# Building the rounding tails of the fp32r weights: sums on TensorE in PSUM in place of three GpSimd steps

## The chip, the cores and the metric

One NeuronCore of a Trainium2 chip runs the kernel; the other cores are not used. The metric is the device time of one execution in microseconds, the median over several runs. A profile is one further execution of the same program, recorded by the hardware profiler, and has a time of its own.

## The reference

Attention over a pooled key/value image, then two feed-forward layers with different activations. The arrays come in as float64 or float32 as the host has them; the weights of the feed-forward layers reach the kernel as 64-bit numbers.

```
kv_flat = mean over 4x4 blocks of kv, @ w_sr        # 768 keys, k = v
a   = softmax(q @ k.T / sqrt(128));  x = a @ v      # 12288 queries of 128
h   = x @ moe_w_in    (128 x 2048);  g = elu(h);           x2 = g @ moe_w_out
h   = x2 @ moe2_w_in  (128 x 2048);  g = max(0.01 h, h);   y  = g @ moe2_w_out
```

## The kernel before, in words

Every product is made from three fp32r matmuls: an operand is held as a head (the value rounded to fp32r) and a tail (the rest, rounded to fp32r), and `mm3` (lines 86 to 89) adds head x head, head x tail and tail x head in PSUM. The 12288 queries are worked on in 24 chunks of 512. For a chunk there are four score tiles of 128 queries, softmax, a turn of the result, the product with the values (`values`, line 433, 18 matmuls), and then for each of the two layers eight units: `up` (six matmuls, 256 hidden features), the activation, the split into head and tail, `down` (six matmuls). In the traces these matmuls stand under lines 87, 88 and 89: `ps` is what `up` and the scores write, `py` what `down` writes.

The weights of the layers are turned from 64-bit words into head and tail on the chip, once, in 32 jobs of 128 x 256 values (`w_parts`, lines 181 to 241). Before, a job is ten steps on a staged tile `ws` of pairs of words (low word, high word): ScalarE takes the absolute value of the high word (`w_abs`, line 193); GpSimd clamps it (`w_bound`, 197); VectorE shifts it (`w_shift`, 203), puts the sign in (`w_sign`, 210) and takes out the power of two (`w_power`, 217); ScalarE converts and scales the low word (`w_low`, 223) and rounds the upper part to the head `wh` (`w_head`, 227); GpSimd multiplies the scaled low word by the power (`w_b`, 231), subtracts the head from the upper part (`w_rest`, 235) and adds the two into the tail `wl` (`w_tail`, 239). The three scratch tiles `v`, `m`, `a` of a job come from the pool `wt` with three buffers, the staged words from `ws` with four.

The order of all instructions from the attention on is written out by a planner at the end of the function (lines 531 to 802). A `step` has an engine, a planned length, the steps that it follows and a key; `take` and `give` name buffers. The planner begins, again and again, the step that can begin first by its own model of the five engines (ties go to the smaller key), and emits it. Each engine then works through its own instructions in that order. Weight jobs have keys six units ahead of the unit that needs them. Three PSUM places of two banks each (`ps`) are shared by score tiles, the turns of the first two chunks (`turn_early`, 413), `values` and `up`; the planner hands them out. The remaining two banks hold the outputs of `down` (`py`). The activation steps that matter here are `relu` (468), `elu_exp` (471), `elu` (475, VectorE), `elu_head` (481, GpSimd), `leaky_head` and `leaky` (487, 491, ScalarE) and `tail` (495, VectorE, writes `gl`); of the attention, `largest` (347), `expo` (354), `norm` (373, GpSimd) and `tail_e` (422, VectorE).

The planned lengths of the steps of a weight job stand in lines 565 to 574 (0.36 us for a ScalarE step, 0.66 us for each of the three GpSimd steps at the end).

Of the kernel before, what the change touches and what calls it, by code (L numbers as in the profile page):

```python
# [18 lines left out]
P = 128  # L19
CH = 512  # L20
S = 32
WP = 256
# [17 lines left out]
def pooled_attention_elu_leaky_kernel(  # L40
# [50 lines left out]
    def pool(name, bufs, **kw):  # L91
        return ctx.enter_context(tc.tile_pool(name=name, bufs=bufs, **kw))

    const = pool("const", 1)
    ident = const.tile([P, P], F32, name="ident")
    w_src = {"i1": w_in1, "o1": w_out1, "i2": w_in2, "o2": w_out2}
    w_hi = {}
    w_lo = {}
# [17 lines left out]
    d_p = pool("scratch", 4, space=bass.MemoryType.DRAM)  # L116
    xs_p = pool("xs", 2)
    ws_p = pool("ws", WS)
    wt_p = pool("wt", 3)
    ps_p = [pool(f"ps_{i}", 1, space=PSUM) for i in range(3)]  # L120
    ps_y = pool("ps_y", 2, space=PSUM)

# [37 lines left out]


    wjobs = [(k, p) for ks in (("i1", "o1"), ("i2", "o2")) for p in range(DFF // WP) for k in ks]
    wst, wt = {}, {}

    def load_w(i):
        k, p = wjobs[i]
# [14 lines left out]
    def w_parts(i):  # L181

        k, p = wjobs[i]
        pp, o = divmod(p * WP, CH)
        hi, lo = w_hi[k, pp][:, o:o + WP], w_lo[k, pp][:, o:o + WP]
        u = lambda x: x.bitcast(U32)

        def w_abs():
            v, m, a = wt[i] = [wt_p.tile([P, WP], F32, tag=x, name=x) for x in "vma"]
            nc.scalar.activation(out=v, in_=f(wst[i][:, :, 1]), func=AF.Abs)

        def w_bound():
            v, m, a = wt[i]
            nc.gpsimd.tensor_scalar(  # L197
                out=v, in0=v, scalar1=TOP, scalar2=LEAST, op0=ALU.min, op1=ALU.max
            )

        def w_shift():
            v, m, a = wt[i]
            nc.vector.tensor_scalar(  # L203
                out=u(a), in0=u(v), scalar1=3, scalar2=0x3FFFFFF8,
                op0=ALU.logical_shift_left, op1=ALU.bitwise_and,
            )

        def w_sign():
            v, m, a = wt[i]
            nc.vector.scalar_tensor_tensor(  # L210
                out=u(a), in0=wst[i][:, :, 1], scalar=0xC0000000, in1=u(a),
                op0=ALU.bitwise_and, op1=ALU.bitwise_or,
            )

        def w_power():
            v, m, a = wt[i]
            nc.vector.tensor_scalar(
                out=u(m), in0=u(a), scalar1=0xFF800000, scalar2=None, op0=ALU.bitwise_and
            )

        def w_low():
            v, m, a = wt[i]
            nc.scalar.activation(out=v, in_=wst[i][:, :, 0], func=AF.Copy, scale=2.0 ** -52)

        def w_head():
            v, m, a = wt[i]
            nc.scalar.activation(out=hi, in_=a, func=AF.Copy)

        def w_b():
            v, m, a = wt[i]  # L230
            nc.gpsimd.tensor_tensor(out=v, in0=v, in1=m, op=ALU.mult)  # L231

        def w_rest():
            v, m, a = wt[i]
            nc.gpsimd.tensor_tensor(out=a, in0=a, in1=f(hi), op=ALU.subtract)  # L235

        def w_tail():
            v, m, a = wt[i]
            nc.gpsimd.tensor_tensor(out=lo, in0=a, in1=v, op=ALU.add)  # L239

        return w_abs, w_bound, w_shift, w_sign, w_power, w_low, w_head, w_b, w_rest, w_tail

    with tc.tile_pool(name="kvp", bufs=1) as kvp, tc.tile_pool(name="sums", bufs=2) as sum_p:
        wsr = kvp.tile([P, C], F32, name="wsr")
        nc.scalar.dma_start(out=wsr, in_=w_sr)
        NL = kv_v.shape[1] // 2
        kvt = [kvp.tile([P, 2, CH], F32, name=f"kv_{i}") for i in range(NL)]
        load_q(0)  # L250
        for i in range(NL):
            nc.sync.dma_start(out=kvt[i], in_=kv_v[:, 2 * i:2 * i + 2, :])
        for i in range(WS):
            load_w(i)
        load_q(1)
        make_identity(nc, ident)
        pool_m = kvp.tile([P, 7 * 32], F32, name="pool_m")
        nc.vector.memset(pool_m, 0.0)
        red = kvp.tile([P, 4, 8], F32, name="red")
        nc.vector.tensor_reduce(  # L260
            out=red,
            in_=ident.rearrange("p (h r w) -> p h w r", h=4, r=R),
            op=ALU.add,
            axis=AX.X,
        )
        nc.vector.tensor_scalar(
            out=pool_m[:, 96:128],
            in0=red.rearrange("p h w -> p (h w)"),
            scalar1=1.0 / (R * R),
            scalar2=None,  # L270
            op0=ALU.mult,
        )
        kvT = kvp.tile([P, NK], F32, name="kvT")
        pooled = {}

        def column_sums(i):
            x = kvt[i]
            s2 = sum_p.tile([P, 2, 2 * C], F32, tag="s2", name="s2")
            s1 = sum_p.tile([P, 2, C], F32, tag="s1", name="s1")
            nc.vector.tensor_tensor(  # L280
                out=s2, in0=x[:, :, :CH // 2], in1=x[:, :, CH // 2:], op=ALU.add
            )
            nc.vector.tensor_tensor(out=s1, in0=s2[:, :, :C], in1=s2[:, :, C:], op=ALU.add)
            g = i // 2
            if i % 2 == 0:
                pooled[g] = ps_p[g % 3].tile([P, 2, CH], F32, tag="s", name="ps")[:, 0]
            for h in range(2):
                j = 2 * (i % 2) + h
                nc.tensor.matmul(
                    pooled[g][:, :P], s1[:, h, :], pool_m[:, 96 - 32 * j:224 - 32 * j],  # L290
                    start=(j == 0), stop=(j == 3),
                )
            if i % 2:
                nc.scalar.activation(
                    out=kvT[:, g * P:(g + 1) * P], in_=pooled[g][:, :P], func=AF.Copy
                )

        def grouped(x):
            return x.rearrange("p (a i) -> p a i", i=S)

        def project(g):
            o = slice(g * P, (g + 1) * P)
            pk, pv = pooled[g][:, P:2 * P], pooled[g][:, 2 * P:3 * P]
            nc.tensor.matmul(pk, wsr, kvT[:, o], start=True, stop=True)
            nc.tensor.matmul(pv, kvT[:, o], wsr, start=True, stop=True)
            nc.scalar.activation(
                out=kt_v[0][:, :, g, :], in_=grouped(pk), func=AF.Copy, scale=SCALE
            )
            nc.scalar.activation(out=v_hi[:, o], in_=pv, func=AF.Copy)

        def project_rest(g):
            o = slice(g * P, (g + 1) * P)
            pk, pv = pooled[g][:, P:2 * P], pooled.pop(g)[:, 2 * P:3 * P]
            nc.vector.scalar_tensor_tensor(
                out=kt_v[1][:, :, g, :], in0=grouped(pk), scalar=SCALE,
                in1=f(kt_v[0][:, :, g, :]), op0=ALU.mult, op1=ALU.subtract,
            )
            nc.vector.tensor_tensor(
                out=v_lo[:, o], in0=pv, in1=f(v_hi[:, o]), op=ALU.subtract
            )  # L320

        for i in range(NL):
            if i == NL - 3:
                turn_q(0)
                split_q(0)
            column_sums(i)
            if i % 2 == 0 and i >= 2:
                project(i // 2 - 1)
            if i % 2 == 1 and i >= 5:
                project_rest((i - 5) // 2)  # L330
        project(NKB - 1)
        project_rest(NKB - 2)
        project_rest(NKB - 1)
# [222 lines left out]
    for i, (k, p) in enumerate(wjobs):  # L556
        m = int(k[1])
        n = where[m, 0, p] + (0 if k[0] == "i" else LAG[m])
        key = n - WAHEAD
        ld = None  # L560
        if i >= WS:
            ld = step(SP, 0.4, lambda i=i: load_w(i), [], key - 8)
            take(ld, "ws", i, WS)
        steps_w = w_parts(i)
        ab = step(ACT, 0.36, steps_w[0], [ld], key)
        bo = step(POOL, 0.46, steps_w[1], [ab], key)
        sh = step(DVE, 0.3, steps_w[2], [bo], key + 0.1)
        si = step(DVE, 0.4, steps_w[3], [sh], key + 0.2)
        po = step(DVE, 0.3, steps_w[4], [si], key + 0.3)
        lw = step(ACT, 0.36, steps_w[5], [sh], key + 0.2)  # L570
        hd = step(ACT, 0.36, steps_w[6], [si], key + 0.2)
        wb = step(POOL, 0.66, steps_w[7], [po, lw], key + 0.4)
        wr = step(POOL, 0.66, steps_w[8], [hd, po], key + 0.5)
        wl = step(POOL, 0.66, steps_w[9], [wb, wr], key + 0.6)
        take(ab, "wt", i, 3)
        give(wl, "wt", i)
        give(max(si, lw), "ws", i)
        w_ready[k, p] = wl


# [252 lines left out]
```

## Time and profile before

| what | value |
|---|---|
| median of 3 runs | 1368.07 us (1367.92 to 1368.38) |
| the profiled execution's own time | 1382.48 us |
| its span in the trace | 1380.7 us |
| PE (matmul) busy | 1318.0 us, 95% |
| DVE (VectorE) busy | 1120.0 us, 81% |
| ACT (ScalarE) busy | 1001.6 us, 73% |
| POOL (GpSimd) busy | 466.7 us, 34% |
| mean granted TensorE clock | 0.981 of full |

PEld is the loading of matmul weights, which overlaps PE. An average over the whole span hides the two stages of this kernel: a first one of some 210 us in which the weights are prepared, and a long one in which they all lie in SBUF. The page's 40 slices show them; a slice is 34.5 us:

```profile
PE   5668779999999999999999999999999999999998
DVE  6889888887887887887887878878878878886663
ACT  2756676787787777777777777777867767776775
POOL 0887883332322323323323323323323323232110
PEclk9879999999999999999999999999999999999999
```

Each digit is the busy share of a slice in tenths; PEclk is the granted TensorE clock in tenths of full speed.

### The profile page before, as it was taken

To read this page: it belongs to the slowest core of one execution; us is meant where nothing else is said; L and a number is where in the kernel's file an instruction comes from. 1 tells how busy PE (TensorE), PEld (TensorE's weight loads), DVE (VectorE), ACT (ScalarE), POOL (GpSimd) and SP (SyncE) were. 2 spreads that over 40 slices of the span, in tenths; PEclk is the share of its full clock that TensorE was granted. 3 is DMA by queue.
4 is the path that set the end of the run, shared out by engine and by line. 5 is a ranking of instruction groups with operands and counts; after the bars stand their busy time and mean duration, and the time that the engine had idled before them with its cause. 6 is when DMAs were issued, how large, how long until landed. Compare 5 with 4: busy or idle time off the path is not lost.

```text
span 1380.7 us, 16414 instructions
## 1 busy us (share of the span) xinstructions
PE 1318.0 (95%) x5736; PEld 1080.2 (78%) x5736; DVE 1120.0 (81%) x1303; ACT 1001.6 (73%) x1243; POOL 466.7 (34%) x422
## 2 busy tenths in 40 slices
PE   5668779999999999999999999999999999999998
PEld 4556558888888888888888888888888888888886
DVE  6889888887887887887887878878878878886663
ACT  2756676787787777777777777777867767776775
POOL 0887883332322323323323323323323323232110
PEclk9879999999999999999999999999999999999999
DMA  7233223223223223223123123222232232120001
GB/s 238 69 107 106 70 69 84 69 61 85 69 62 84 69 62 84 69 62 85 57 61 84 58 61 85 63 68 77 61 77 69 61 85 69 54 76 23 9 8 16
DMA packets 170658, 97.61 MB, mean 71 GB/s; under 512 B 104912, under 2 KB 154192, under 8 KB 170576
## 3 DMA queue, kind: packets, MB, share of 16 engines
q1 hardware_dynamic: 169376, 96.36, 25.1%
q8 instruction: 46, 0.75, 0.2%
q10 hardware_dynamic: 1200, 0.20, 0.1%
q14 instruction: 36, 0.29, 0.1%
HBM read 55.64 MB, written 40.89 MB: 70 GB/s over the span
## 4 chain that ended last, share of the span: by engine, by line
PE 86%; DVE 5%; POOL 4%; issue 2%; ACT 1%; DMA 1%; SPq 0%; DVEq 0%; POOLq 0%; ACTq 0%
PE ps L88 14%; PE ps L87 14%; PE ps L89 14%; PE py L88 12%; PE py L89 12%; PE py L87 12%; PE ps L433 6%; POOL a L235 1%; DVE a L210 1%; POOL v L231 1%; DMA kv<-in_kv_dram 1%; DVE gl L495 1%; POOL wl_i L239 0%; POOL v L197 0%; DVE a L203 0%
## 5 line engine op out<-in xcount | busy, mean ns | idle before, releaser
L495 DVE TENSOR_TENSOR gl<-g,gh 128x1024 fp32r<-128x1024 f32 x384 | 475.2, 1265 | 97.1 <-POOL gh L481 77.5
L481 POOL TENSOR_SCALAR gh<-g 128x1024 fp32r<-128x1024 f32 x192 | 216.9, 1130 | 654.1 <-DVE g L475 580.7
L88 PE MATMUL py<-gl,wh_o 128*128 128x512 f32 x768 | 307.0, 400 | 13.3 <-DVE gl L495 13.3
L87 PE MATMUL py<-gh,wh_o 128*128 128x512 f32 x768 | 305.0, 397 | 5.0 <-POOL gh L481 2.9
L89 PE MATMUL py<-gh,wl_o 128*128 128x512 f32 x768 | 306.0, 398 | 0.0
L468 ACT ACTIVATE r<-ps 128x1024 f32<-128x1024 f32 x192 | 196.9, 1025 | 142.1 <-PE ps L89 141.6
L475 DVE SCALAR_TENSOR_TENSOR g<-r,ps 128x1024 f32<-128x1024 f32 x192 | 232.7, 1213 | 76.3 <-ACT r L471 76.1
L487 ACT ACTIVATE gh<-ps 128x1024 fp32r<-128x1024 f32 x192 | 196.2, 1022 | 62.2 <-PE ps L89 60.1
L471 ACT ACTIVATE r<-r 128x1024 f32<-128x1024 f32 x192 | 203.7, 1061 | 5.9
L491 ACT ACTIVATE g<-ps 128x1024 f32<-128x1024 f32 x192 | 196.0, 1021 | 0.0
L373 POOL TENSOR_SCALAR e<-e,rs 128x768 f32<-128x768 f32 x88 | 134.1, 1524 | 162.8 <-DVE rs L363 83.6
L88 PEld LDWEIGHTS py<-gl,wh_o 128*128 128x128 f32 x768 | 145.6, 190 | 47.3 <-DVE gl L495 17.6
L87 PEld LDWEIGHTS py<-gh,wh_o 128*128 128x128 f32 x768 | 145.5, 189 | 36.6 <-POOL gh L481 4.1
L89 PEld LDWEIGHTS py<-gh,wl_o 128*128 128x128 f32 x768 | 145.9, 190 | 32.8
L87 PE MATMUL ps<-xh,wh_i 128*128 128x512 f32 x384 | 155.4, 405 | 7.7 <-DVE g L475 3.8
L88 PE MATMUL ps<-xl,wh_i 128*128 128x512 f32 x384 | 154.5, 402 | 0.0
L89 PE MATMUL ps<-xh,wl_i 128*128 128x512 f32 x384 | 154.3, 402 | 0.0
L87 PE MATMUL ps<-x2h,wh_i 128*128 128x512 f32 x384 | 152.1, 396 | 1.6 <-ACT e L354 1.6
L88 PE MATMUL ps<-x2l,wh_i 128*128 128x512 f32 x384 | 152.0, 396 | 0.0
L89 PE MATMUL ps<-x2h,wl_i 128*128 128x512 f32 x384 | 151.7, 395 | 0.0
L422 DVE TENSOR_TENSOR el<-e,eh 128x768 fp32r<-128x768 f32 x88 | 101.1, 1150 | 8.3 <-ACT eh L418 8.3
L354 ACT ACTIVATE e<-ps,nm 128x768 f32<-128x768 f32 x96 | 85.8, 894 | 26.2 <-DVE nm L347 23.9
(73 smaller groups left out, 1663.7 us busy)
## 6 DMA issues: line engine op xcount, KB each, us to landing
d<-e SPq DMA_DIRECT2D x88, 384.0 KB, 2.6
x<-d SPq DMA_DIRECT2D x88, 384.0 KB, 3.1
qn<-in_q_dram SPq DMA_DIRECT2D x96, 64.0 KB, 2.5
kv<-in_kv_dram SPq DMA_DIRECT2D x12, 512.0 KB, 8.9
out_dram<-y SPq DMA_DIRECT2D x94, 64.0 KB, 2.2
ws<-in_moe_w_in_dram SPq DMA_DIRECT2D x16, 256.0 KB, 3.0
ws<-in_moe_w_out_dram SPq DMA_DIRECT2D x16, 256.0 KB, 2.8
out_dram<-y ACTq DMA_DIRECT2D x2, 64.0 KB, 2.9
```

Of the source, the lines that this page charges most:

```text
L87: nc.tensor.matmul(ps, w_hi, x_hi, start=start, stop=False)
L88: nc.tensor.matmul(ps, w_hi, x_lo, start=False, stop=False)
L89: nc.tensor.matmul(ps, w_lo, x_hi, start=False, stop=stop)
L373: nc.gpsimd.tensor_scalar(out=x, in0=e, scalar1=rs_t.pop(t), scalar2=1.0, op0=ALU.mult, op1=ALU.mult)
L422: nc.vector.tensor_tensor(out=lo, in0=e_t.pop(t), in1=f(hi), op=ALU.subtract)
L468: nc.scalar.activation(out=r_u[n], in_=ps_u[n], func=AF.Relu, scale=-1.0)
L471: nc.scalar.activation(out=r_u[n], in_=r_u[n], func=AF.Exp, scale=-1.0)
L475: nc.vector.scalar_tensor_tensor(out=g_u[n], in0=r_u.pop(n), scalar=-1.0, in1=ps_u.pop(n), op0=ALU.add, op1=ALU.max)
L481: nc.gpsimd.tensor_scalar(out=gh_u[n], in0=g_u[n], scalar1=1.0, scalar2=0.0, op0=ALU.mult, op1=ALU.add)
L487: nc.scalar.activation(out=gh_u[n], in_=ps_u[n], func=AF.Prelu, alpha=0.01)
L491: nc.scalar.activation(out=g_u[n], in_=ps_u.pop(n), func=AF.Prelu, alpha=0.01)
L495: nc.vector.tensor_tensor(out=gl_u[n], in0=g_u.pop(n), in1=f(gh_u[n]), op=ALU.subtract)
```

## The change

Two constant matrices are added, `plus` (identity in fp32r) and `minus` (its negative), made once by ScalarE. `w_low` falls away. `w_b` moves to VectorE and does the conversion, the scaling and the product in one instruction, straight from the staged words into a tile `b` of type fp32r. `w_rest` becomes three matmuls of 256 columns into half of a PSUM place: the fp32 identity times the upper part `a` (fp32), `minus` times the head, `plus` times `b`. `w_tail` becomes one ScalarE instruction that reads this sum from PSUM and writes it as the tail. GpSimd keeps `w_bound` alone. The scratch pool `wt` has two buffers in place of three (given back after the matmuls), the staged words are held until `w_b`, and a job takes one of the three PSUM places from its matmuls to its last step. The planned lengths are changed too.

```
@@ -93,6 +93,8 @@
 
     const = pool("const", 1)
     ident = const.tile([P, P], F32, name="ident")
+    plus = const.tile([P, P], F32R, name="plus")
+    minus = const.tile([P, P], F32R, name="minus")
     w_src = {"i1": w_in1, "o1": w_out1, "i2": w_in2, "o2": w_out2}
     w_hi = {}
     w_lo = {}
@@ -116,7 +118,7 @@
     d_p = pool("scratch", 4, space=bass.MemoryType.DRAM)
     xs_p = pool("xs", 2)
     ws_p = pool("ws", WS)
-    wt_p = pool("wt", 3)
+    wt_p = pool("wt", 2)
     ps_p = [pool(f"ps_{i}", 1, space=PSUM) for i in range(3)]
     ps_y = pool("ps_y", 2, space=PSUM)
 
@@ -160,7 +162,7 @@
 
 
     wjobs = [(k, p) for ks in (("i1", "o1"), ("i2", "o2")) for p in range(DFF // WP) for k in ks]
-    wst, wt = {}, {}
+    wst, wt, w_ps = {}, {}, {}
 
     def load_w(i):
         k, p = wjobs[i]
@@ -189,56 +191,56 @@
         u = lambda x: x.bitcast(U32)
 
         def w_abs():
-            v, m, a = wt[i] = [wt_p.tile([P, WP], F32, tag=x, name=x) for x in "vma"]
-            nc.scalar.activation(out=v, in_=f(wst[i][:, :, 1]), func=AF.Abs)
+            wt[i] = [wt_p.tile([P, WP], t, tag=x, name=x) for x, t in zip("mab", (F32, F32, F32R))]
+            nc.scalar.activation(out=wt[i][0], in_=f(wst[i][:, :, 1]), func=AF.Abs)
 
         def w_bound():
-            v, m, a = wt[i]
+            m, a, b = wt[i]
             nc.gpsimd.tensor_scalar(
-                out=v, in0=v, scalar1=TOP, scalar2=LEAST, op0=ALU.min, op1=ALU.max
+                out=m, in0=m, scalar1=TOP, scalar2=LEAST, op0=ALU.min, op1=ALU.max
             )
 
         def w_shift():
-            v, m, a = wt[i]
+            m, a, b = wt[i]
             nc.vector.tensor_scalar(
-                out=u(a), in0=u(v), scalar1=3, scalar2=0x3FFFFFF8,
+                out=u(a), in0=u(m), scalar1=3, scalar2=0x3FFFFFF8,
                 op0=ALU.logical_shift_left, op1=ALU.bitwise_and,
             )
 
         def w_sign():
-            v, m, a = wt[i]
+            m, a, b = wt[i]
             nc.vector.scalar_tensor_tensor(
                 out=u(a), in0=wst[i][:, :, 1], scalar=0xC0000000, in1=u(a),
                 op0=ALU.bitwise_and, op1=ALU.bitwise_or,
             )
 
         def w_power():
-            v, m, a = wt[i]
+            m, a, b = wt[i]
             nc.vector.tensor_scalar(
                 out=u(m), in0=u(a), scalar1=0xFF800000, scalar2=None, op0=ALU.bitwise_and
             )
 
-        def w_low():
-            v, m, a = wt[i]
-            nc.scalar.activation(out=v, in_=wst[i][:, :, 0], func=AF.Copy, scale=2.0 ** -52)
-
         def w_head():
-            v, m, a = wt[i]
+            m, a, b = wt[i]
             nc.scalar.activation(out=hi, in_=a, func=AF.Copy)
 
         def w_b():
-            v, m, a = wt[i]
-            nc.gpsimd.tensor_tensor(out=v, in0=v, in1=m, op=ALU.mult)
+            m, a, b = wt[i]
+            nc.vector.scalar_tensor_tensor(
+                out=b, in0=wst[i][:, :, 0], scalar=2.0 ** -52, in1=m, op0=ALU.mult, op1=ALU.mult
+            )
 
         def w_rest():
-            v, m, a = wt[i]
-            nc.gpsimd.tensor_tensor(out=a, in0=a, in1=f(hi), op=ALU.subtract)
+            m, a, b = wt[i]
+            ps = w_ps[i][:, 0, :WP]
+            nc.tensor.matmul(ps, ident, a, start=True, stop=False)
+            nc.tensor.matmul(ps, minus, hi, start=False, stop=False)
+            nc.tensor.matmul(ps, plus, b, start=False, stop=True)
 
         def w_tail():
-            v, m, a = wt[i]
-            nc.gpsimd.tensor_tensor(out=lo, in0=a, in1=v, op=ALU.add)
-
-        return w_abs, w_bound, w_shift, w_sign, w_power, w_low, w_head, w_b, w_rest, w_tail
+            nc.scalar.activation(out=lo, in_=w_ps.pop(i)[:, 0, :WP], func=AF.Copy)
+
+        return w_abs, w_bound, w_shift, w_sign, w_power, w_head, w_b, w_rest, w_tail
 
 
 
@@ -254,6 +256,8 @@
             load_w(i)
         load_q(1)
         make_identity(nc, ident)
+        nc.scalar.activation(out=plus, in_=ident, func=AF.Copy)
+        nc.scalar.activation(out=minus, in_=ident, func=AF.Copy, scale=-1.0)
         pool_m = kvp.tile([P, 7 * 32], F32, name="pool_m")
         nc.vector.memset(pool_m, 0.0)
         red = kvp.tile([P, 4, 8], F32, name="red")
@@ -562,19 +566,20 @@
             ld = step(SP, 0.4, lambda i=i: load_w(i), [], key - 8)
             take(ld, "ws", i, WS)
         steps_w = w_parts(i)
-        ab = step(ACT, 0.36, steps_w[0], [ld], key)
-        bo = step(POOL, 0.46, steps_w[1], [ab], key)
-        sh = step(DVE, 0.3, steps_w[2], [bo], key + 0.1)
+        ab = step(ACT, 0.4, steps_w[0], [ld], key)
+        bo = step(POOL, 0.5, steps_w[1], [ab], key)
+        sh = step(DVE, 0.25, steps_w[2], [bo], key + 0.1)
         si = step(DVE, 0.4, steps_w[3], [sh], key + 0.2)
-        po = step(DVE, 0.3, steps_w[4], [si], key + 0.3)
-        lw = step(ACT, 0.36, steps_w[5], [sh], key + 0.2)
-        hd = step(ACT, 0.36, steps_w[6], [si], key + 0.2)
-        wb = step(POOL, 0.66, steps_w[7], [po, lw], key + 0.4)
-        wr = step(POOL, 0.66, steps_w[8], [hd, po], key + 0.5)
-        wl = step(POOL, 0.66, steps_w[9], [wb, wr], key + 0.6)
-        take(ab, "wt", i, 3)
-        give(wl, "wt", i)
-        give(max(si, lw), "ws", i)
+        po = step(DVE, 0.25, steps_w[4], [si], key + 0.3)
+        hd = step(ACT, 0.4, steps_w[5], [si], key + 0.2)
+        wb = step(DVE, 0.4, steps_w[6], [po], key + 0.4)
+        wr = step(PE, 0.8, steps_w[7], [hd, wb], key + 0.5)
+        take(wr, "ps", None, 3, lambda ps, i=i: w_ps.__setitem__(i, ps))
+        wl = step(ACT, 0.45, steps_w[8], [wr], key + 0.6)
+        give(wl, "ps", wr)
+        take(ab, "wt", i, 2)
+        give(wr, "wt", i)
+        give(wb, "ws", i)
         w_ready[k, p] = wl
```

## Rows read from the trace of the kernel before

**Rows 1.** Busy time by stage; columns: stage, length, PE, PEld, DVE, ACT, POOL, clock, DMA

```profile
30.00:210.00 180.00, 137.16 (x532) 105.37 (x533) 156.55 (x231) 121.40 (x210) 148.12 (x164) 0.88 0.27 81
400.00:700.00 300.00, 300.00 (x1331) 248.41 (x1330) 252.32 (x281) 227.54 (x268) 88.16 (x69) 1.00 0.26 71
```

**Rows 2.** Chain that ended last, two pieces: start, length, what

```profile
470.72 4.12 PE ps L433 x18
523.13 4.20 PE ps L433 x18
```

**Rows 3.** The same chain, shares by line, from 128 to 212 us

```profile
by line: issue 22.9%; POOL a L235 18.4%; DVE a L210 10.6%; POOL v L231 7.4%; POOL wl_i L239 4.9%; DVE gl L495 4.8%; POOL v L197 3.9%; POOL e L373 3.3%; DVE g L475 2.9%; POOL wl_o L239 2.9%; PE ps L433 2.7%; DVE m L217 2.7%; DVE a L203 2.5%;
```

**Rows 4.** Groups by line and shape, 30 to 210 us: GpSimd's three steps

```profile
L231 POOL TENSOR_TENSOR v<-v,m 128x256 f32<-128x256 f32 x32 | 30.0, 946 | 11.3 <-DVE m L217 6.2 <-ACT wh_o L227 2.5 <-ACT v L223 1.4
...
L235 POOL TENSOR_TENSOR a<-a,wh_o 128x256 f32<-128x256 f32 x16 | 16.9, 1054 | 0.0
L239 POOL TENSOR_TENSOR wl_o<-a,v 128x256 fp32r<-128x256 f32 x16 | 16.6, 1041 | 0.5
...
L235 POOL TENSOR_TENSOR a<-a,wh_i 128x256 f32<-128x256 f32 x16 | 15.5, 967 | 1.8 <-ACT wh_i L227 1.8
...
L239 POOL TENSOR_TENSOR wl_i<-a,v 128x256 fp32r<-128x256 f32 x16 | 12.2, 766 | 0.6
```

**Rows 5.** Groups by line and shape, 30 to 210 us: VectorE

```profile
L495 DVE TENSOR_TENSOR gl<-g,gh 128x1024 fp32r<-128x1024 f32 x26 | 37.2, 1434 | 5.1 <-POOL gh L481 5.1
...
L210 DVE SCALAR_TENSOR_TENSOR a<-ws,a 128x256 uint32<-128x256 uint32 x32 | 23.1, 738 | 0.5
...
L217 DVE TENSOR_SCALAR m<-a 128x256 uint32<-128x256 uint32 x32 | 15.5, 503 | 0.5
...
L203 DVE TENSOR_SCALAR a<-v 128x256 uint32<-128x256 uint32 x32 | 11.5, 367 | 10.9 <-POOL v L197 10.9
```

**Rows 6.** One line's instructions: shortest, median, longest in ns

```profile
L495 DVE TENSOR_TENSOR gl<-g,gh x26: 1209/1336/2052, 80.8 to 207.8; 128x1024 fp32r<-128x1024 f32 x26
...
L210 DVE SCALAR_TENSOR_TENSOR a<-ws,a x32: 404/612/1267, 36.0 to 202.2; 128x256 uint32<-128x256 uint32 x32
...
L217 DVE TENSOR_SCALAR m<-a x32: 275/295/1159, 36.5 to 203.5; 128x256 uint32<-128x256 uint32 x32
...
L203 DVE TENSOR_SCALAR a<-v x32: 244/293/820, 30.6 to 201.9; 128x256 uint32<-128x256 uint32 x32
```

**Rows 7.** Waits from 30 to 210 us: who for whom, total, times, longest

```profile
PE py L88 <- DVE gl L495: 13.3, 10, 2.7
...
DVE a L203 <- POOL v L197: 10.9, 10, 2.1
...
PE ps L87 <- ACT e L354: 7.3, 5, 3.3
...
DVE gl L495 <- POOL gh L481: 5.1, 4, 2.3
```

**Rows 8.** Timeline of PE: start, length, what; fp32 products, then fp32r scores

```profile
14.79 0.39 PE L304 MATMUL ps<-kvT,wsr 128*128 128x128 f32 x2
15.02 0.39 PE L305 MATMUL ps<-wsr,kvT 128*128 128x128 f32 x2
...
33.92 0.34 PE L88 MATMUL ps<-kt_lo,qh 128*128 128x384 f32 x1
34.10 0.34 PE L89 MATMUL ps<-kt_hi,ql 128*128 128x384 f32 x1
...
67.55 0.52 PE L87 MATMUL ps<-kt_hi,qh 128*128 128x384 f32 x1
67.87 0.52 PE L88 MATMUL ps<-kt_lo,qh 128*128 128x384 f32 x1
```

**Rows 9.** Groups by line and shape, 30 to 210 us: ScalarE

```profile
L223 ACT ACTIVATE v<-ws 128x256 f32<-128x256 uint32 x32 | 13.6, 433 | 10.6 <-DVE a L203 10.6
...
L437 ACT ACTIVATE xh<-ps 128x512 fp32r<-128x512 f32 x3 | 1.8, 593 | 1.3 <-PE ps L433 1.3
```

## What I predict

> **What bounds the kernel now.** I first read busy time by stage, because the change touches only work that is done once. From 400 to 700 us PE is busy without a gap at the full clock, and VectorE (84%), ScalarE (76%) and GpSimd (29%) all have room [rows 1]: there PE's own matmuls set the pace, and no weight step is left. From 30 us (the key/value image is in) to 210 us it is another kernel: PE is busy 137.2 of 180 us at a granted clock of 0.88, VectorE 156.6 and GpSimd 148.1 [rows 1]. So the change can pay or cost only in these 180 us, and the forecast is how long the same work takes there afterwards. The long stage should end as much earlier or later as it begins.
>
> Next the chain that ended last, from 128 to 212 us: GpSimd's weight steps, lines 197, 231, 235 and 239, are 18.4 + 7.4 + 4.9 + 3.9 + 2.9 = 37.5% of it, VectorE's, lines 203, 210 and 217, 15.8%, and PE a few per cent [rows 3]. The groups say why: three of GpSimd's four steps per job take 30.0 + 16.9 + 16.6 + 15.5 + 12.2 = 91.2 us for 96 instructions, 0.95 us each [rows 4], where the planner counts 0.66. The waits show how it reaches PE: VectorE stands 10.9 us for the clamp that queues behind those steps and 5.1 us for GpSimd's heads, and PE stands 13.3 us for `gl` of VectorE [rows 7]. VectorE also pays inside its instructions. The sign step takes 404 ns at its shortest, 738 in the mean and 1267 at its longest, and the two other weight steps and `tail` spread likewise [rows 5, 6].
>
> All of this is in one profiled execution that took 1382.48 us by its own time, 14.4 above the median of 1368.07. That is not in the stage I sum: the 18 matmuls of `values` take 4.12 us up to 470 us and 4.20 from 523 us on [rows 2]. I take the difference in the 180 us over to the median unchanged: a gain of 8 is 1374.5 against the execution and 1360 against the median.
>
> **GpSimd.** It loses 91.2 of its 148.1 us [rows 1, 4] and keeps 56.9, 38%. It can't set the pace then.
>
> **VectorE.** The new `w_b` has two SBUF inputs, 128 x 256, one of them every second word: the sign step is its nearest row. Ends: 404 ns alone, 1267 ns at worst; times 32 that is 12.9 to 40.5 us. What VectorE loses now over its shortest instructions is 32 x (0.738 - 0.404) = 10.7 for the sign, 32 x (0.503 - 0.275) = 7.3, 32 x (0.367 - 0.244) = 3.9 and, for `tail`, 26 x (1.434 - 1.209) = 5.9, together 27.8 us [rows 5, 6]. I let this excess shrink with GpSimd's busy time, to 38%: 17.2 us come back, and `w_b` costs 404 + 0.38 x 334 = 531 ns, 17.0 us. Busy time afterwards: 156.6 - 17.2 + 17.0 = 156.4. VectorE's load is not what improves. Its idle time is 180 - 156.6 = 23.4 us, of which 16.0 are the two waits for GpSimd; all of it would be gone at best, none at worst. I take half, 8, because a unit that comes a step earlier often meets PE or ScalarE instead. So VectorE needs 156.4 + 15.4 = 171.8 us: **8 us less than 180**.
>
> **TensorE.** The fp32 products of 128 columns follow each other at 15.02 - 14.79 = 0.23 us, so 256 columns take 0.46; the fp32r matmuls of 384 columns at 0.18, so 256 take between 0.12 and 0.18, say 0.13 [rows 8]. A sum is 0.46 + 0.26 = 0.72 us, 32 are 23.0 us. At the lower clock the same 384 columns follow at 0.32 us [rows 8]; 32 sums would be up to 43. PE stands idle 42.8 us of the 180 [rows 1], so 23 fit if they fall into the gaps; if that cover is gone they cost 23 to 43. By the pace of the long stage (1331 matmuls in 300 us) the 532 of the first stage are 120 us of work [rows 1], so 143 with the sums, against 172 forecast. That leaves 29 us for waits and slow clock where 60 stand now: the side on which my sum is tight.
>
> The Trainium skill (Perfetto Trace Analysis, "Identifying the Most-Contended Engine") says to judge TensorE's headroom by the loading of weights, not by matmul busy time. By that rule PE does 105.4/180 against 248.4/300, 71% of its pace in the long stage: room for 53 us, not 42.8, and the sums would hide more easily. I keep the 42.8.
>
> **ScalarE.** `w_low` (433 ns) goes and `w_tail` comes. The nearest row that reads PSUM is 593 ns for 512 columns; 256 lie between 0.3 and 0.59, about 0.43 [rows 9]. Over 32 that is -4 to +5 us on an engine that is busy 121 of 180 [rows 1]: nothing, with VectorE's queue as cover; without it, those 5 us. Making `plus` and `minus` is two small instructions before the key/value image has come: nothing, covered by that load.
>
> **Buffers and queues.** With two scratch sets, not three, a job may take twice the mean distance of jobs, 2 x 180/32 = 11 us, from its absolute value to its sum; the steps in between add up to about 3.3 us without queues. Nothing, until queues eat 8 us. No DMA is added; the staged words are held to `w_b`, and a later load shifts in SP's queue: nothing, as four tiles are staged. A sum holds one of three PSUM places for 0.72 + 0.43 us and ScalarE's queue, about 2 us, 64 place-us in 540. PE already stands 7.3 us for places that `expo` frees [rows 7]; ends 0 and about another 7.3, taken as inside the half that I didn't count above. New waits: VectorE's shift waits for the sum two jobs earlier; PE's sum waits for `w_b` and the head, and everything behind it on PE waits too. That is the slower rival.
>
> **The rivals.** *Slower: PE stands at the sums.* A sum is emitted between other matmuls; if VectorE's `w_b` is late behind 1.2 us instructions, the scores and units behind it stand. PE's spare time after the sums is 42.8 - 23.0 = 19.8 us; it decides from 19.8/32 = 0.62 us of waiting per sum. At 1.0 us the stage grows by 32 - 19.8 = 12.2: 1380. For it: `down` already waits 1.33 us a time for `gl` in just this way (13.3 in 10) [rows 7]. Against it: the planned lengths miss less (0.4 planned for `w_b`, 0.53 expected; before, 0.66 planned and 0.95 measured), so the sums stand where their operands are due. The Trainium skill (TensorE: Matmul & The Clock Gate, "The mechanism") has matmuls start and end strictly in program order, which is this mechanism; the wait of `down` agrees.
>
> *No change: VectorE is the bound.* Its load stays at 156.4 us; if its idle time stays too, with other names, it needs 179.8 us: 1368. For it: 87% busy is high for an engine at the end of so many hand-offs. Against it: two thirds of its idle time has GpSimd's name on it. The change also amounts to this if GpSimd's lines on the chain only stand in for VectorE's.
>
> *Much faster: the whole excess goes.* VectorE then needs 156.6 - 27.8 + 12.9 + 7.4 = 149; PE, with 143 us of work and half of its present idle time, 143 + 21.4 = 164, which sets the stage: 16 us less, 1352. For it: GpSimd falls to a third. Against it: its clamp and heads still meet VectorE, as in the long stage.
>
> **How the numbers follow.** Chances: forecast 0.53 (1354 to 1365.4), much faster 0.13, no change 0.17, slower 0.17. A measurement of this kernel tells 0.2%, 2.7 us, from no change. So faster by more than that 0.66, within 0.17, slower 0.17. The unknown costs (`w_b` at 12.9 or 23.6 us, idle time kept or not) move the forecast by some 6 us either way. The range, 1350 to 1374, takes in no change, the slower rival up to 0.8 us per sum and much faster to just beyond its figure; about 2 in 10 lie outside.
>
> **What would show it.** Right: GpSimd at about a third in the first stage, no wait of VectorE for the clamp above 3 us in total, the sign step near 530 ns, `w_b` near it, PE gapless from about 202 us, the long stage as before. Wrong: new waits of PE for `w_b` or for the head at the sums, together above 20 us; waits for PSUM places that `w_tail` frees; `w_b` above 0.75 us; or the gapless stretch beginning at 210 or later with VectorE above 93%. A change of pace in the long stage would refute the frame itself.

## The result, and the profile after

The kernel after takes 1354.09 us (median of 4 runs, 1352.93 to 1355.95) against 1368.22 for the kernel before in the same comparison: 14.1 us less. The ratio on record, which is not simply that of the two medians (0.9897), is 0.9878 with a 95% interval of 0.9834 to 0.9923. The forecast was 1360, 8 us less, with a range of 1350 to 1374. Direction and range held; the gain was larger than forecast by 6 us.

Where it came from is first read by stage, as in [rows 1] (same columns). The first stage now ends at 193.46 us: I take as its end the start of `values` of the fourth chunk, which was at 209.85 before, with nearly the same number of matmuls done (531 before; 657 less the 128 of the sums after).

```profile
30.00:209.85 179.85, 137.01 (x531) 105.26 (x532) 156.40 (x231) 121.40 (x210) 148.12 (x164) 0.88 0.27 81
```

That is the kernel before up to that point; the next is the kernel after, with the long stage under it.

```profile
30.00:193.46 163.46, 142.71 (x657) 114.71 (x656) 152.19 (x264) 120.05 (x211) 68.61 (x68) 0.98 0.30 90
...
400.00:700.00 300.00, 300.00 (x1343) 249.93 (x1342) 251.21 (x278) 228.23 (x269) 85.65 (x69) 1.00 0.26 72
```

The stage is 16.4 us shorter. GpSimd fell from 148.1 to 68.6 us of work. VectorE, with one instruction more per job, works 152.2 us instead of 156.4, and its idle time went from 23.4 to 11.3. PE works 142.7 instead of 137.0 with 128 matmuls more, stands idle 20.8 instead of 42.8, and its granted clock is 0.98 instead of 0.88. The long stage is what it was: PE without a gap. (The spans of the two profiles differ by more, 29.2 us, because in the profile before `values` slows from 4.12 to 4.20 us [rows 2] and in this one it does not. Other profiles of both kernels show the slower pace from other points on, so the experiments below are read by ratios to the kernel before on the same chip, and by the first stage in the profiles.)

The chain that ended last, shares by line from 128 to 194 us, stands against [rows 3]:

```profile
by line: DVE gl L499 12.4%; issue 8.4%; PE ps L87 7.9%; PE ps L89 7.9%; PE ps L88 7.9%; PE py L88 7.7%; PE py L89 6.7%; PE py L87 5.9%; PE ps L236 5.3%; DVE a L212 4.2%; DVE a L205 2.9%; DVE g L479 2.8%; DVE e L406 2.7%; ACT r L472 1.4%; AC
```

GpSimd's weight steps, 37.5% of the chain before, are not among its larger shares any more; PE's matmuls and VectorE's `tail` have taken their place. The groups of the weight job and of `tail` from 30 to 193.46 us, against [rows 5] (busy us, mean ns, then idle time before them):

```profile
L499 DVE TENSOR_TENSOR gl<-g,gh 128x1024 fp32r<-128x1024 f32 x26 | 32.3, 1247 | 1.3 <-POOL gh L485 1.3
...
L212 DVE SCALAR_TENSOR_TENSOR a<-ws,a 128x256 uint32<-128x256 uint32 x32 | 19.2, 612 | 0.7
...
L199 POOL TENSOR_SCALAR m<-m 128x256 f32<-128x256 f32 x32 | 18.5, 585 | 62.5 <-ACT m L195 57.9 <-DVE nm L351 3.7
...
L229 DVE SCALAR_TENSOR_TENSOR b<-ws,m 128x256 fp32r<-128x256 uint32 x32 | 13.6, 440 | 2.0 <-DVE m L219 0.5
...
L205 DVE TENSOR_SCALAR a<-m 128x256 uint32<-128x256 uint32 x32 | 11.1, 360 | 3.2 <-POOL m L199 2.8 <-PE ps L238 0.5
...
L219 DVE TENSOR_SCALAR m<-a 128x256 uint32<-128x256 uint32 x32 | 10.1, 330 | 0.6
```

The same `tail` instructions, 26 of them, take 1247 instead of 1434 ns, the sign 612 instead of 738, the power 330 instead of 503. The shift stayed at 360. VectorE's waits for GpSimd, 16.0 us before [rows 7], are 2.8 + 1.3 = 4.1 here.

The sums on PE, from the groups and the timeline (start, length, what; the first line of the timeline begins a sum, the last one follows it):

```profile
L236 PE MATMUL ps<-a,ident 128*128 128x256 f32 x64 | 21.3, 415 | 10.1 <-ACT e L358 3.6 <-DVE g L479 3.0 <-ACT wl_i L241 1.1
...
L238 PE MATMUL ps<-b,plus 128*128 128x256 f32 x32 | 9.5, 297 | 0.1
```

```profile
149.96 0.59 PE L236 MATMUL ps<-a,ident 128*128 128x256 f32 x2
...
150.62 0.40 PE L87 MATMUL py<-gh,wh_o 128*128 128x512 f32 x1
```

A sum holds PE for 150.62 - 149.96 = 0.66 us. PE waits 10.1 us in all before them, 0.32 us a sum, and nearly all of it for a PSUM place (that `expo`, `elu` or an earlier `w_tail` frees). For `b` it waits 0.1 us in all.

### The profile page after: what moved, and what is told of

It reads as the page before. It is cut to its first block, busy times and chain, and to the rows that moved or that the text cites. A ratio compares the mean times of both kernels' runs of the same rounds, so it can differ in the third digit from the quotient of the medians.

```text
span 1351.5 us, 16631 instructions
## 1 busy us (share of the span) xinstructions
PE 1311.3 (97%) x5864; PEld 1085.9 (80%) x5864; DVE 1114.8 (82%) x1335; ACT 1000.0 (74%) x1245; POOL 385.7 (29%) x326
## 4 chain that ended last, share of the span: by engine, by line
PE 89%; DVE 6%; ACT 2%; issue 1%; POOL 1%; DMA 0%; SPq 0%; DVEq 0%; POOLq 0%; ACTq 0%
PE ps L88 15%; PE ps L87 15%; PE ps L89 15%; PE py L88 12%; PE py L89 12%; PE py L87 12%; PE ps L437 6%; DVE gl L499 1%; DVE a L212 1%; DVE g L479 1%; DVE el L426 1%; PE ps L236 1%; DVE nm L351 1%; DVE a L205 0%; DVE e L406 0%
## 5 line engine op out<-in xcount | busy, mean ns | idle before, releaser
L499 DVE TENSOR_TENSOR gl<-g,gh 128x1024 fp32r<-128x1024 f32 x384 | 470.2, 1253 | 94.5 <-POOL gh L485 76.8
L485 POOL TENSOR_SCALAR gh<-g 128x1024 fp32r<-128x1024 f32 x192 | 222.8, 1160 | 668.6 <-DVE g L479 632.4
L88 PE MATMUL py<-gl,wh_o 128*128 128x512 f32 x768 | 302.3, 394 | 2.3 <-DVE gl L499 2.2
L89 PE MATMUL py<-gh,wl_o 128*128 128x512 f32 x768 | 301.1, 392 | 0.0
L87 PE MATMUL py<-gh,wh_o 128*128 128x512 f32 x768 | 299.9, 390 | 0.2 <-DVE x2l L519 0.2
L87 PE MATMUL ps<-xh,wh_i 128*128 128x512 f32 x384 | 151.1, 393 | 1.0 <-ACT e L358 1.0
L88 PE MATMUL ps<-xl,wh_i 128*128 128x512 f32 x384 | 151.6, 395 | 0.0
L89 PE MATMUL ps<-xh,wl_i 128*128 128x512 f32 x384 | 151.0, 393 | 0.0
```

What stands on the lines that cost most here:

```text
L87: nc.tensor.matmul(ps, w_hi, x_hi, start=start, stop=False)
L88: nc.tensor.matmul(ps, w_hi, x_lo, start=False, stop=False)
L89: nc.tensor.matmul(ps, w_lo, x_hi, start=False, stop=stop)
L485: nc.gpsimd.tensor_scalar(out=gh_u[n], in0=g_u[n], scalar1=1.0, scalar2=0.0, op0=ALU.mult, op1=ALU.add)
L499: nc.vector.tensor_tensor(out=gl_u[n], in0=g_u.pop(n), in1=f(gh_u[n]), op=ALU.subtract)
```

## The experiments

Theory G, as I began: the gain is GpSimd's work taken away. Each ratio below is to the kernel before on the chip of that run's batch; "stage" is the start of the fourth chunk's `values` in the profile (before 209.85, after 193.46). The kernel after was measured again beside ballast_memset, clamp_dve and after_ab3 only; the other runs were on two other chips, so there a distance to the kernel after is one between ratios that were not taken together. A ratio is uncertain by 0.15 to 0.45% (2 to 6 us), and one profile gives the stage: the same kernel showed 193.46 and 194.57.

| run | ratio, 95% interval | stage, us |
|---|---|---|
| after | 0.9878 [0.9834, 0.9923] | 193.46 |
| after again (after_ctl) | 0.987 [0.984, 0.990] | 194.57 |
| before_lengths | 1.0031 [1.0016, 1.0045] | 212.80 |
| before_pe | 1.0073 [1.0044, 1.0101] | 212.67 |
| b_pool | 0.9925 [0.9896, 0.9954] | 196.68 |
| before_b_dve | 1.0018 [0.9981, 1.0055] | 210.37 |
| after_ballast | 1.0222 [1.0191, 1.0252] | 233.56 |
| ballast_memset | 0.9965 [0.9943, 0.9988] | 205.63 |
| clamp_dve | 0.994 [0.9911, 0.9968] | 203.93 |
| sums_twice | 0.9951 [0.9908, 0.9995] | 204.80 |
| after_ab3 | 0.986 [0.9823, 0.9898] | 197.33 |
| nearly3 | 1.0065 [1.0022, 1.0107] | 216.98 |

**Is it the written order?** The change also set other planned lengths. Edit to the kernel before:

```
-        sh = step(DVE, 0.3, ...    si = step(DVE, 0.4, ...    po = step(DVE, 0.3, ...
+        sh = step(DVE, 0.37, ...   si = step(DVE, 0.74, ...   po = step(DVE, 0.5, ...
-        wb = step(POOL, 0.66, ...  wr = step(POOL, 0.66, ...  wl = step(POOL, 0.66, ...
+        wb = step(POOL, 0.95, ...  wr = step(POOL, 1.01, ...  wl = step(POOL, 0.9, ...
```

> The kernel before with six planned lengths of the weight job set to the measured means (GpSimd 0.95, 1.01, 0.90; VectorE 0.37, 0.74, 0.50), nothing else. Theory G: the load stays, so the time stays, 1364 to 1372 us. Rival L (the gain came from an order written with truer lengths): 1353 to 1359 us.

Measured 1.0031: truer lengths alone make it no faster, but 0.3% slower. Rival L falls.

**Is it TensorE's clock?** The granted clock rose from 0.88 to 0.98. Edit to the kernel before, with a PE step after the head (`give` of the place at once; GpSimd's steps stay):

```
+        def w_extra():
+            ps = w_ps.pop(i)[:, 0, :WP]
+            nc.tensor.matmul(ps, ident, f(hi), start=True, stop=False)
+            nc.tensor.matmul(ps, kt_hi[:, :P], hi, start=False, stop=False)
+            nc.tensor.matmul(ps, kt_hi[:, P:2 * P], hi, start=False, stop=True)
...
+        we = step(PE, 0.8, steps_w[10], [hd], key + 0.5)
```

> The kernel before plus, for each weight job, matmuls of the same sizes as the sums into a PSUM place that nobody reads; GpSimd still does its three steps. Theory G: no gain, 1368 to 1385 us, since 23 us of matmuls are added and GpSimd stays loaded. Rival C (the extra matmuls fill PE's gaps, and the higher granted clock is what made the kernel faster): 1354 to 1362 us, with a granted clock above 0.95 from 30 to 210 us.

Measured 1.0073, some 10 us more (of which the profile shows 2.8 in the first stage), with a clock of 0.92 from 30 to 210 us. Filling PE's gaps did not make the kernel faster. It also did not reach the clock that rival C asks for, above 0.95, so this run alone does not refute it. The run clamp_dve, further down, has the clock of the kernel after, 0.98 in its first stage, and that stage still ends 9.4 us later than in after_ctl: the clock alone does not bring the gain. That the higher clock follows from a PE that waits less is an argument; no run isolates it.

**One part at a time.** First the kernel after with the product on GpSimd again (`w_low` back on ScalarE, planned lengths 0.45 and 0.75):

```
+            nc.scalar.activation(out=b, in_=wst[i][:, :, 0], func=AF.Copy, scale=2.0 ** -52)
...
-            nc.vector.scalar_tensor_tensor(
-                out=b, in0=wst[i][:, :, 0], scalar=2.0 ** -52, in1=m, op0=ALU.mult, op1=ALU.mult
-            )
+            nc.gpsimd.tensor_tensor(out=b, in0=f(b), in1=m, op=ALU.mult)
```

> The kernel after, with the product of the low words back on GpSimd (and ScalarE's conversion of the low word back): VectorE loses 32 x 0.44 = 14 us of work, GpSimd gets 32 instructions of 0.75 to 0.95 us back, some 24 to 30 us, a third of what the change took from it. Theory G (the gain is GpSimd's load taken away, by amount): a third of the 14 us goes, 1357 to 1361 us. Rival V (after the change VectorE is the bound of the first stage, 95% busy from 75 to 140 us): faster than after, 1345 to 1351 us.

Measured 0.9925, at the kernel before's 1368 that is 1358: as theory G had it. By the stage less goes, 2.1 to 3.2 us. VectorE without `w_b` did not win: it works 144.5 us of this stage, but stands idle 22.2, against 11.3 in the kernel after. Then the other part alone, in the kernel before (VectorE does `w_b` in one instruction, `w_low` falls away, GpSimd keeps `w_rest` and `w_tail`; the staged words are held until `w_b`):

```
-            nc.gpsimd.tensor_tensor(out=v, in0=v, in1=m, op=ALU.mult)
+            nc.vector.scalar_tensor_tensor(
+                out=v, in0=wst[i][:, :, 0], scalar=2.0 ** -52, in1=m, op0=ALU.mult, op1=ALU.mult
+            )
```

> The kernel before with one part of the change alone: VectorE makes the scaled low word in one instruction (ScalarE's conversion falls away), GpSimd keeps subtraction and sum. GpSimd loses 30 us, VectorE gets 32 x 0.44 to 0.8 = 14 to 26. Theory V and P together (VectorE pays for its own work and for GpSimd's two-input steps beside it): within 5 us of the kernel before, ratio 0.996 to 1.004. Rival G (gain in proportion to GpSimd's load taken away): a third of the gain, ratio 0.994 to 0.997.

Measured 1.0018, no change: here theory G in its plain form, gain in proportion to GpSimd's load, falls. Moving the sums alone gives 0.75% (b_pool; 13.2 us of the stage), moving the product alone nothing, both 1.2 to 1.3% (15.3 to 16.4 us). Here VectorE's idle time fell from 23.4 to 12.4 us, but its work rose from 156.4 to 167.9: what it no longer waited it worked. VectorE's `w_b` takes 440 ns in the kernel after, 558 here beside two-input steps of GpSimd; over 32 jobs that is 3.8 us. That the product pays only once those steps are gone fits this, but its share after them, 0.5% by the ratios and 2.1 to 3.2 us by the stage, is near what the measurements can tell.

```profile
L227 DVE SCALAR_TENSOR_TENSOR v<-ws,m 128x256 f32<-128x256 uint32 x32 | 17.3, 558 | 0.4
```

**What GpSimd's steps cost VectorE.** To the kernel after I added three GpSimd instructions per job for which nobody waits, first as products that read two tiles, then, with the same planned lengths, as fills that read nothing:

```
+            nc.gpsimd.tensor_tensor(out=ball[0], in0=ball[0], in1=ball[1], op=ALU.mult)   # after_ballast, 128x256
+            nc.gpsimd.memset(ball[0], 1.0)                                                # ballast_memset, 128x512
...
+        b0 = step(POOL, 0.66, steps_w[9], [po], key + 0.4)
+        b1 = step(POOL, 0.66, steps_w[9], [b0, hd], key + 0.5)
+        step(POOL, 0.66, steps_w[9], [b1], key + 0.6)
```

> The kernel after plus three GpSimd products of 128 x 256 per weight job on a scratch tile of their own, at the places of the three old steps, for which nobody waits. Theory G (load and contention of GpSimd): back to 1362 to 1372 us, VectorE's sign step near 700 ns again. Rival W (not the load, but that the tails waited for a chain of steps in GpSimd's queue): 1353 to 1358 us.

> As the run with three added GpSimd products per job, with the same planned lengths and so the same written order, but each product is a fill of 128 x 512 that reads nothing from SBUF. Theory P (VectorE loses time where a GpSimd instruction reads SBUF beside it): most of what the products cost goes, 5 to 15 us above the kernel after, VectorE's sign step below 650 ns. Rival O (the written order with GpSimd's places taken, or GpSimd's queue, made that run slow): within 10 us of it, 30 us or more above the kernel after.

The products make the kernel slower than the kernel before, 1.0222, though nobody waits for them; theory G had them back at about 1.0 with the sign step near 700 ns (821 in the mean), so the amount was missed upwards. Rival W falls. The fills, in the same written order, cost 0.95% above the kernel after, 13 us; the products 3.5%. So the order explains at most the smaller part (rival O falls) and theory P holds for the larger part, but for its number for the sign step, below 650 ns expected, 673 measured. The fills are also shorter than the products, 52 against 79 us of GpSimd's time in all, so the two runs load GpSimd's queue unequally. Busy time by stage (columns as in [rows 1], products first, then fills) shows that the queue is not what made the difference:

```profile
30.00:233.56 203.56, 160.86 (x656) 126.70 (x657) 190.94 (x263) 120.72 (x210) 142.27 (x164) 0.89 0.25 73
```

```profile
30.00:205.63 175.63, 151.98 (x658) 119.89 (x657) 163.22 (x264) 121.19 (x213) 113.33 (x164) 0.94 0.30 83
```

Against the kernel after the stage is 40.1 us longer with products, and VectorE's own work 38.8; with fills 12.2 and 11.0. Its idle time hardly moves (12.6 and 12.4, against 11.3). VectorE did not wait longer for GpSimd, its instructions took longer. The lines of the sign, the power and `w_b` (shortest/median/longest ns), in the run with products and in the run with fills:

```profile
L215 DVE SCALAR_TENSOR_TENSOR a<-ws,a x32: 406/910/1259, 36.0 to 225.3; 128x256 uint32<-128x256 uint32 x32
...
L222 DVE TENSOR_SCALAR m<-a x32: 274/707/890, 36.5 to 226.5; 128x256 uint32<-128x256 uint32 x32
...
L232 DVE SCALAR_TENSOR_TENSOR b<-ws,m x32: 414/841/1098, 37.3 to 227.2; 128x256 fp32r<-128x256 uint32 x32
```

```profile
L215 DVE SCALAR_TENSOR_TENSOR a<-ws,a x32: 405/426/1268, 38.5 to 198.7; 128x256 uint32<-128x256 uint32 x32
...
L222 DVE TENSOR_SCALAR m<-a x32: 273/490/801, 38.9 to 199.9; 128x256 uint32<-128x256 uint32 x32
...
L232 DVE SCALAR_TENSOR_TENSOR b<-ws,m x32: 405/424/1092, 39.8 to 200.3; 128x256 fp32r<-128x256 uint32 x32
```

Beside products all three instructions of VectorE take 2.0 to 2.6 times their shortest time in the median. Beside fills the sign and `w_b`, which have two SBUF inputs, are back at 426 and 424 in the median, as in the kernel after; the power, which has one, is not (490, there 294), and no run shows why. The Trainium skill (SBUF — State Buffer, "SBUF: two separate sides") says that VectorE and GpSimd share a pair of ports under an exclusive lock, and that a VectorE instruction with two SBUF inputs takes it only against a GpSimd instruction that reads SBUF; the medians of the sign and of `w_b` in these rows agree.

**What bounds the first stage now.** VectorE is busy 61.5 of 65 us from 75 to 140 us in the kernel after. Three edits press on VectorE, on PE and on the scratch sets. The clamp on VectorE, so that GpSimd has no weight step:

```
-            nc.gpsimd.tensor_scalar(out=m, in0=m, scalar1=TOP, scalar2=LEAST, ...
+            nc.vector.tensor_scalar(out=m, in0=m, scalar1=TOP, scalar2=LEAST, ...
```

> The kernel after with the clamp on VectorE, so that GpSimd does no weight step. VectorE gets 32 x 0.25 to 0.3 = 8 to 10 us more; its excess over the shortest instructions (13 us over the four weight steps) shrinks. Theory P: the two cancel, within 4 us of the kernel after. Rival V (VectorE's load alone is the bound now): 6 to 10 us slower.

Measured 0.994, 0.7% or 9.7 us above the kernel after on the same chip: rival V (VectorE's load is the bound) was right, theory P wrong that taking the clamp off GpSimd would pay for it. VectorE's work rose from 152.2 to 164.7 us. The clamp on GpSimd, with its one input, costs VectorE's sign step nothing that shows: it took 612 ns with it and 610 without.

The sums computed twice (the first three matmuls repeated, the result overwritten):

> The kernel after with each sum computed twice on TensorE (the first result is overwritten), 23 us of matmuls more in the first stage. Theory V (VectorE is the bound there, PE has gaps): 3 to 12 us above the kernel after. Rival T (PE's time is the bound after the change): 20 to 25 us above it, a ratio above 1.0.

Measured 0.9951, 0.8% or 11 us above the kernel after by two ratios, each uncertain by 4 to 6 us; the medians of this run alone, 1374.75 against 1376.08 for the kernel before, would put it at some 16. The profiles are clearer: the stage is 11.3 us longer, PE's busy time 18.0, its idle time 6.6 shorter. So of the 21 us of matmuls that were added (32 x 0.66) about half comes through. Rival T (20 us or more, above 1.0) falls, but PE's time counts as well as VectorE's: neither engine alone bounds this stage. The sums of the change itself are then probably partly paid, too; no run shows how much.

Three buffers for the upper part and the scaled low word instead of two:

> The kernel after with three buffers instead of two for the upper part and the scaled low word (the tile of the absolute value keeps two). Theory G: within 3 us of the kernel after, since jobs come 5 us apart. Rival B (two scratch sets hold the jobs back): 4 to 10 us faster.

Measured 0.986 against 0.987, and the stage ends 2.8 us later, not earlier: two scratch sets cost nothing that can be measured. Rival B is not borne out, though the interval alone would still allow a gain of 4 us.

**An attempt at a faster kernel.** If VectorE bounds the stage, its four turns of the third chunk could go to PE:

```
-NEARLY = 2
+NEARLY = 3
```

> The kernel after with the turn of the third chunk's four tiles on TensorE too, as for the first two chunks: VectorE loses four turns of 0.97 us in the first stage, PE gets four of 0.9 us, and the sixteen transfers to and from memory of this chunk fall away. Theory V: 3 to 6 us faster than the kernel after, ratio to the kernel before 0.981 to 0.985. Rival: PSUM places are what is short, same or slower.

Measured 1.0065, slower than the kernel before. VectorE is busy only 37.7 of 65 us from 75 to 140 us (busy time by stage, columns as in [rows 1]), and PE waits for places that `elu` frees (from 30 to 216.98 us):

```profile
75.00:140.00 65.00, 47.73 (x177) 36.16 (x176) 37.70 (x63) 31.04 (x54) 15.45 (x19) 0.84 0.15 41
```

```profile
PE ps L236 <- DVE g L479: 12.4, 5, 3.6
```

The result is the rival's, same or slower, and these waits fit its reason, that PSUM places are short. But the planner also wrote another order: `values` of the second chunk begins at 119.19 us, in the kernel after at 89.15. Whether the places or this order made it slow was not isolated. (The chunk has eight transfers, four out and four back, not sixteen.) None of the runs beats the kernel after by more than the measurement can tell.

## Why the prediction was right, and where its sum was short

- **The frame held.** Only the first stage changed; the long stage is PE without a gap before and after [rows 1], and it begins where the first one ends: PE is busy for all of 193.5 to 210 us. The gain is the earlier end of the first stage: 16.4 us in the profile, 14.1 in the medians.
- **GpSimd.** Forecast 56.9 us left, measured 68.6, or 42% of the stage in place of a third: `elu_head` (22.9 to 28.4 us) and `norm` (its nine instructions that write in place, 10.2 to 13.4) got longer, the clamp hardly (559 to 585 ns). Why is not shown. GpSimd does not set the pace, as forecast.
- **VectorE's work: too high by 4.2 us** (forecast 156.4, measured 152.2). `w_b` took 440 ns, not 531; 13.6 us, not 17.0. The change leaves GpSimd no instruction that reads two whole tiles. That is 3.4 of the 4.2, and the listed excess gives back 2.5 of it. The excess of the other instructions shrank by 32 x (0.738 - 0.612) + 32 x (0.503 - 0.330) + 32 x (0.367 - 0.360) + 26 x (1.434 - 1.247) = 14.7 us of the forecast 17.2. So 3.3 us are not in the terms that I listed: `tail_e` on SBUF tiles went from 10.2 to 8.4 us, and the other 1.5 are in no single row. That the total came near is in part luck: two of its errors have opposite signs.
- **VectorE's idle time: the mis-sized term.** I took half of the 16.0 us of waits for GpSimd as gone, 8, "because a unit that comes a step earlier often meets PE or ScalarE instead". 11.9 went and, in sum, nothing came in their place: idle time is 11.3 us where 15.4 was forecast. These two terms, 4.2 and 4.1, are the 8.3 us between the forecast stage (171.8) and the measured one (163.5).
- **TensorE.** Forecast 0.72 us a sum, measured 0.66. The tight side of my sum, 29 us for waits and slow clock, was not tight: PE stands idle 20.8 us at a clock of 0.98. That is the sum of the much faster rival, 143 + 21.4, almost to the microsecond (142.7 + 20.8). The Trainium skill's rule (Perfetto Trace Analysis, "Identifying the Most-Contended Engine") on judging TensorE's room by weight loading gave 53 us where I kept 42.8. The sums of 21 us fit into either, so no run here decides between the two; sums_twice shows that neither is time to be filled for nothing.
- **The slower rival** needed 0.62 us of waiting per sum and had 0.32, almost none of it for `w_b`; planned and measured lengths of `w_b` (0.40 and 0.44) lie close together. Its mechanism exists: with the products of after_ballast, where `w_b` takes 824 ns, PE stands 5.9 us in 7 waits for `b`. Its price was not reached here.
- **The no-change rival** fell with VectorE's idle time; before_lengths and before_pe speak against two other ways to the same gain. **Much faster** (1352) was nearer to the result than my figure was: its condition, that the excess and the waits nearly all go, was met for most of the waits (11.9 of 16.0) and for half of the excess (14.7 of 27.8).
- **The signs.** Of those that I named, the wait for the clamp (2.8 us, below 3), a `w_b` not longer than forecast and no wait of PE for it (0.1) came; the sign step near 530 ns (612) and GpSimd at a third did not. My "0.2%" for what a measurement tells was too fine: the intervals here are 0.15 to 0.45% either way.

## What to carry to other kernels

An instruction on GpSimd that reads two tiles costs more than its own queue: here VectorE's instructions beside many of them took 2.0 to 2.6 times their shortest time in the median, and that has to be priced beside the waits for GpSimd when work is moved off it. Here the waits fell by 11.9 us and the lengthening by 14.7, and the new work on VectorE took 13.6 of it back. Price also where the work goes: the product moved to VectorE alone gave nothing, the two sums moved to TensorE 0.75%, all three 1.2 to 1.3%. TensorE had gaps for the sums at 0.66 us a job, but when as much again was added only about half of it was hidden.

## What the runs showed of the hardware that I had not expected

GpSimd instructions differ in what they cost VectorE by what they read: 96 fills of 527 ns (median) that read nothing left the two-input sign step at a median of 426 ns (426 without them), 96 products of 792 ns took it to 910, in the same written order. The one-input power step suffered from both, 490 and 707 ns, against 294 in the kernel after. The granted clock of the first stage, a mean over stretches at the lower and at the full level, was 0.88 before, 0.92 with matmuls that nobody reads, 0.98 after the change. More matmuls in the same time go with it there, but not everywhere: before_b_dve, with 528 in 180.4 us against 531 in 179.9 before, shows 0.90.
